# Long FFT convolution feeding a phase mixer: phase steps, evictions and transfers re-placed around the last inverse transform

## The chip, the cores and the metric

The kernel runs on one core of a Trainium2 chip. The metric is device time in microseconds of that core, as the median of repeated executions of the whole program. The kernel before was executed eight times: median 2128.61 us, lowest 2123.54, highest 2137.8.

## The reference, cut to what matters

There are two layers. The first is a causal long convolution along the sequence, done with a Fourier transform of twice the length:

```python
batch, seq, d_model = 8, 5696, 128
Y = rfft(x, n=2*seq, axis=1) * rfft(h, n=2*seq, axis=0)
y = irfft(Y, n=2*seq, axis=1)[:, :seq, :]
```

The second takes y as its input. It forms an angle for every token and channel, rotates, mixes the tokens with two seq x seq matrices, and ends with a small channel layer:

```python
theta = y @ w_theta
zr, zi = y * cos(theta), y * sin(theta)
u = y + w_tok_r @ zr + w_tok_i @ zi      # over tokens, per batch and channel
out = u + relu(u @ w_ch)
```

The two token matrices hold 2 x 5696 x 5696 numbers in float32, and every one of them is read from HBM. Inputs and output are float32; inside, the kernel works in f16 (transforms) and bf16 (mixing).

## The kernel before, in words

**Convolution.** The work is cut into eight groups: four pairs of batches (bp) by two halves of the channels (dh). Each group passes four stages. Stages a and b (`stage_a`, `stage_b`) transform forward and multiply with the transform of h; stages c and d (`stage_c`, `stage_d`) transform back. Stage c of a group has 16 chunks of 16 matmuls, each evicted from PSUM into the tile `g`. Stage d has 7 chunks (six of 10 and one of 4 columns), each evicted into the tile `yt` (line 349). When a group's `yt` is whole it is written to HBM as `yt_hbm` (line 355). The loop at line 594 weaves the back transform of one group with the forward transform of the next. The last group has no next one; its place is taken by phase steps.

**Phase steps.** `phase_step(ti, hh)` handles one tile of 128 tokens for four batches (hh is 0 for batches 0 to 3, 1 for batches 4 to 7). It transposes y on TensorE (L569), computes the angle with two rounds of matmuls (L399 to L405), copies y out of PSUM on VectorE (L574), takes absolute value, sine and cosine on ScalarE (L410, L411, L412), multiplies on VectorE (L423, L424), and sends out y (`y2_hbm`, L575) and the two products (`z_hbm`, L441, or for some tokens straight into the mixing operand, L437). The y copies use six slots in turn, the products seven (`zz`). There are 22 steps for hh = 0 (`steps0`) and 22 for hh = 1 (`steps1`). Of `steps0`, ten are woven into stage c of the last group, six into its stage d (lines 598 and 609), and six follow (line 660). `steps1` are woven into the first stretch of the mixing (line 988, `next_steps`).

**What phase steps read.** y of batches 0 to 3 comes back from HBM into `ya0` (line 534). y of batches 4 to 7 goes into `ya1`: three parts from HBM (lines 544 and 546), and the last half of the channels of batches 6 and 7 directly from the last group's `yt` in SBUF, two transfers on SyncE's queue (SP's, line 549). `stage_d` calls this last load (`then`) and directly after it sends the rest of `yt` to HBM on GpSimd's (POOL's) queue.

**Mixing.** 44 tiles of tokens are handled in two passes over the reduction, with seven products per pair of tiles. The first pair (i = 1, 2, 3 in the loop at line 892) is done plainly, with four products. The operand made of z is held in eleven tiles `b0` to `b10`. The first seven are loaded in half from `z_hbm` on POOL's queue (line 639), which waits for the `steps0` that made them; the other half, and tiles 7 and 8, are completed by the direct writes of `steps1` (L437). Tiles 9 and 10 are loaded by `open_mixing` (line 680), after the last of `steps1`, on SP's queue. The token matrices arrive through a ring of six buffers on POOL's queue (L501): `ring["upto"]` says how many loads may be issued, `pump` issues those that may go and whose buffer has been read. Four addends of the first pair (`cs`, `addend`) are read back from `y2_hbm` and `yt_hbm` on SP's queue (lines 810 and 814), and `tc.issue_after` puts them behind the last load of `open_mixing`.

**What sets the order.** Each engine runs its own instructions in one fixed order. A planner in the framework makes that order: the program's order is its priority, but it may bring an instruction forward that it takes to be ready. `tc.issue_after(ins)` adds an edge: what is issued in its block on the same engine comes after `ins`. PSUM holds four buffers of two banks during the convolution and the `steps0`.

Of the kernel before, what the change touches and what calls it, by code (L numbers as in the profile page):

```python
# [22 lines left out]
def kernel(  # L23
# [310 lines left out]
    def stage_d(st, bp, dh, then=None):  # L334
        def chunk(n0, cn):
            if n0 == 0:
                st["yt"] = fg.tile([P, NB, N2], BF16, tag="yt", name="yt")
            g_, yt = st["g"], st["yt"]
            ps = psum()
            nq = 5 if cn == CN else cn  # L340
            for j in range(cn):
                n = n0 + j
                o = ps[:, j // nq, (j % nq) * NB:(j % nq + 1) * NB]
                for ri in range(2):
                    e_ = e_t[:K1, n, ri, :] if n < EN else e_t[:K1, N2 - n, ri, ::-1]
                    nc.tensor.matmul(o, g_[:K1, ri * N2 + n, :], e_, start=(ri == 0), stop=(ri == 1))
            y_out = yt[:, :, n0:n0 + cn].rearrange("p m (a q) -> p m a q", q=nq)
            y_in = ps[:, :cn // nq, :nq * NB].rearrange("p a (q m) -> p m a q", q=nq)
            nc.scalar.activation(y_out, y_in, AF.Copy)
            if n0 + cn == N2:  # L350
                if then is not None:
                    then(yt)
                for e in range(2):
                    t0 = H if then else 0
                    (nc.gpsimd if then else nc.sync).dma_start(
                        yt_hbm[dh * HD:(dh + 1) * HD, 2 * bp + e, t0:],
                        yt[64 * e:64 * e + 64].rearrange("p m n -> p (m n)")[:, t0:])
        return [lambda n0=n0, cn=cn: chunk(n0, cn) for n0, cn in CHN]

    zz_n, ZB = [0], 3  # L360
# [112 lines left out]
    def pump():  # L473

        while (ring["n"] < len(queue) and (ring["n"] < 6 or queue[ring["n"] - 6][0] in ring["read"])
               and ring["n"] < ring["upto"]):
            queue[ring["n"]][1]()
# [6 lines left out]
    def small(at, n):  # L484
        return ring["all"][:, WB + BT + at:WB + BT + at + n]
# [100 lines left out]
    def with_load(step, load):  # L586
        def both():
            step()
            if load:
                ring["upto"] += 1  # L590
                pump()
        return both

    for g, (bp, dh) in enumerate(groups):
        st = {}
        last = g + 1 == len(groups)
        a_, load_, b_ = front(g + 1)
        now = [with_load(steps0.pop(0), 2 < n < 9) for n in range(10)] if last else []
        c_ = stage_c(st, last)
        if dh == 0 and bp + 1 < B // 2:  # L600
            def next_x(bp=bp):
                x16s[bp + 1] = load_x(bp + 1)
            a_ = a_ + [next_x]
        woven((c_, 0.06 if a_ else 0.0, 1.0), (a_, 0.0, 0.35 if dh == 0 else 0.55), now, load_)
        if g + 2 == len(groups):
            xin.close()
            open_phases()
            load_ya0()
        now = [steps0.pop(0) for _ in range(6)] if last else []
        woven(b_, (stage_d(st, bp, dh, load_ya1 if last else None), 0.0, 1.1 if b_ else 1.0), now)  # L610
        if g + 2 == len(groups):
            load_ya1()
            open_ring()
# [59 lines left out]
    def open_mixing():  # L673

        nonlocal bp, cp, wlp, ybp
        pha.close()
        xa.close()
        bp, cp, wlp, ybp = (ctx.enter_context(tc.tile_pool(name=name, bufs=bufs, reuse_waits="tile"))
                            for name, bufs in (("bpool", 1), ("cpool", 1), ("wlpool", 2), ("ybpool", 3)))
        for j in range(len(bts_of[0]), NJ):  # L680
            load_b(0, j, bp, nc.sync)
        spread.extend(bg_phase(t, h) for t in list(range(24, 34)) + [22, 23, 44] + list(range(34, 44)) for h in range(2))
        spread.extend(bg_left(g) for g in range(0, NT, 4))

# [207 lines left out]
    for i, (k, p, tt, j0, s0, nj) in enumerate(stretches):  # L892
# [67 lines left out]
                for n in range(2):  # L960
                    nc.sync.dma_start(wl[n], wl_hbm[:, 22 * n + tt, :])
        if j0 + s0 == (3 if classic else 2) * TJ:
            with tc.issue_after(sides["late"].ins) if p == 0 and tt == 0 else ExitStack():
                cs = [addend(p, n, t, h) for n, (t, h) in enumerate(where)]

        def aside(first_of, second_of):
            nonlocal second
# [20 lines left out]
        if i == 1:  # L988
            for q, (h, s) in enumerate(((0, 0), (0, 1), (1, 0), (1, 1))):
                for n in range(4):  # L990
                    for j in range(TJ):
                        product((held, a)[s], s * TJ + j, j, n, (h,))
                        if (n * TJ + j) % 2:
                            next_steps(1)
                    if n % 2 and q == 1:
                        ring["upto"] += 1
                        pump()
                    if q == 3 and n == 0:
                        ring["upto"] = len(queue)
                        nxt = prepare(2)  # L1000
            continue
        if i == 2:
            for h in range(2):
# [119 lines left out]
```

## Time and profile before

| What | Value |
|---|---|
| median of eight executions | 2128.61 us |
| the profiled execution, its own time | 2125.64 us |
| span of its instructions | 2123.7 us |
| TensorE busy | 1993.8 us (94%) |
| VectorE busy | 1597.9 us (75%) |
| ScalarE busy | 675.2 us (32%) |
| GpSimd busy, mostly issuing transfers | 908.6 us (43%) |
| granted TensorE clock, mean | 0.972 |

Busy time is summed over the span; an engine's share says little about a single stage. The part that this document is about lies between 385 and 535 us from the span's start: last chunks of the seventh group until 391, stage c of the last group from 393 to 423, stage d to 441, the last `steps0` to 452, and the first stretches of the mixing after that. From 540 us on TensorE works nearly without a gap until the end. In a row such as "PE L569 MATMUL ... [3.41 <-DMA ya<-yt]" the bracket is the time for which the engine stood idle before the instruction and what it was waiting for.

### The profile page before, as it was taken

To read this page: it belongs to the slowest core of one execution; us is meant where nothing else is said; L and a number is where in the kernel's file an instruction comes from. 1 tells how busy PE (TensorE), PEld (TensorE's weight loads), DVE (VectorE), ACT (ScalarE), POOL (GpSimd) and SP (SyncE) were. 2 spreads that over 40 slices of the span, in tenths; PEclk is the share of its full clock that TensorE was granted. 3 is DMA by queue.
4 is the path that set the end of the run, shared out by engine and by line. 5 is a ranking of instruction groups with operands and counts; after the bars stand their busy time and mean duration, and the time that the engine had idled before them with its cause. 6 is when DMAs were issued, how large, how long until landed. Compare 5 with 4: busy or idle time off the path is not lost.

```text
span 2123.7 us, 41486 instructions
## 1 busy us (share of the span) xinstructions
PE 1993.8 (94%) x15765; PEld 1113.8 (52%) x15765; DVE 1597.9 (75%) x2880; ACT 675.2 (32%) x997; POOL 908.6 (43%) x1661
## 2 busy tenths in 40 slices
PE   3788889787999999999999998999999999999998
PEld 3787888754444444444444443444444444444444
DVE  7867767776778887888886757677777777686867
ACT  4877877884332333232310000011111111111111
POOL 5301011237344636354556543445444454545450
PEclk8699989999999999999999999999999999999999
DMA  6357464889789989898999879777878787969693
GB/s 138 100 131 172 126 166 130 230 251 241 157 152 179 178 173 168 170 177 172 175 174 163 129 152 262 109 138 142 145 135 152 129 153 129 158 121 159 127 155 90
DMA packets 408264, 334.95 MB, mean 158 GB/s; under 512 B 85927, under 2 KB 358439, under 8 KB 407079
## 3 DMA queue, kind: packets, MB, share of 16 engines
q0 software_dynamic: 225952, 156.72, 51.7%
q1 hardware_dynamic: 176128, 164.05, 26.5%
q10 hardware_dynamic: 5984, 11.54, 1.5%
q8 instruction: 123, 2.02, 0.4%
q14 instruction: 77, 0.63, 0.1%
HBM read 377.11 MB, written 92.49 MB: 221 GB/s over the span
## 4 chain that ended last, share of the span: by engine, by line
PE 67%; DMA 2%; DVE 2%; issue 1%; POOL 0%; ACT 0%; DVEq 0%; ACTq 0%; POOLq 0%
PE m L1060 61%; PE m L982 2%; DMA b<-z_hbm 2%; PE v L789 1%; PE utp L782 1%; DVE c L1067 1%; PE m L1064 1%; PE m L936 0%; PE m L934 0%; PE theta_ps L388 0%; PE tpz L730 0%; DVE wt L702 0%; DMA ring<-in_moe_w_tok_r_dram 0%; POOL ring L501 0%; DMA yT<-yt_hbm 0%
## 5 line engine op out<-in xcount | busy, mean ns | idle before, releaser
L501 POOL DMA_DIRECT2D ring<-in_moe_w_tok_i_dram x720 | 388.5, 546 | 679.6 <-DVE wt L702 605.7
L501 POOL DMA_DIRECT2D ring<-in_moe_w_tok_r_dram x720 | 387.3, 545 | 150.6 <-DVE wt L702 88.8
L702 DVE STREAM_TRANSPOSE wt<-ring 128x384 f32<-128x384 f32 (+2 forms) x720 | 360.4, 528 | 103.1 <-PE m L1060 70.7
L1060 PE MATMUL m<-b,wt 128*128 128x512 bf16 x1640 | 388.3, 379 | 2.0 <-DVE wt L702 1.7
L1060 PEld LDWEIGHTS <-wt 128*128 128x128 bf16 x1804 | 176.1, 98 | 215.8 <-DVE wt L702 4.4
L1067 DVE TENSOR_TENSOR c<-c,m 128x512 f32<-128x512 f32 x412 | 267.5, 676 | 0.4 <-PE m L1060 0.4
L784 ACT ACTIVATE ring<-utp 128x512 bf16<-128x512 bf16 (+1 forms) x86 | 51.0, 593 | 608.6 <-PE utp L782 608.6
L323 PE MATMUL ps<-r_u,u_t 128*128 128x128 f16 x1024 | 132.2, 229 | 10.5 <-DVE u_t L307 9.9
L324 PE MATMUL ps<-r_v,v_t 128*128 128x128 f16 x1024 | 131.2, 228 | 0.1
L982 PE MATMUL m<-b,wt 128*128 128x512 bf16 x480 | 112.2, 383 | 10.6 <-DMA b<-zz 6.2
L779 ACT ACTIVATE ub<-c 128x512 bf16<-128x512 f32 (+1 forms) x90 | 56.3, 629 | 198.0 <-DVE c L950 116.2
L129 POOL DMA_DIRECT2D x<-in_x_dram x64 | 34.0, 538 | 189.2 <-PE ps L193 178.5
L323 PEld LDWEIGHTS <-u_t 128*128 128x128 f16 x1024 | 106.2, 104 | 11.9 <-DVE u_t L307 11.9
L324 PEld LDWEIGHTS <-v_t 128*128 128x128 f16 x1024 | 105.3, 103 | 2.9 <-DVE v_t L307 1.3
L305 ACT ACTIVATE xs<-ps 128x1024 f16<-128x1024 f32 x96 | 95.3, 1019 | 13.7 <-DVE v_t L307 7.2
L307 DVE TENSOR_TENSOR u_t<-xs,hs 128x1024 f16<-128x1024 f16 x96 | 71.8, 748 | 28.6 <-ACT xs L305 19.3
L193 PE MATMUL ps<-f_t,x 89*128 89x180 f16 x512 | 81.5, 313 | 9.6 <-ACT xs L305 6.7
L982 PEld LDWEIGHTS <-wt 128*128 128x128 bf16 x528 | 50.4, 99 | 70.5 <-issue 15.3
L211 PEld LDWEIGHTS <-w_t 64*128 64x128 f16 x3240 | 60.4, 102 | 39.6 <-issue 25.3
L193 PEld LDWEIGHTS <-x 89*128 89x128 f16 x512 | 73.3, 233 | 11.5 <-issue 10.8
L390 ACT ACTIVATE red<-theta_ps,magic 128x512 f32<-128x512 f32 (+1 forms) x46 | 31.7, 688 | 134.8 <-PE theta_ps L388 113.7
L732 ACT ACTIVATE ring<-tpz 128x512 bf16<-128x512 bf16 (+1 forms) x46 | 27.5, 598 | 136.4 <-PE tpz L730 118.4
(2889 smaller groups left out, 3887.8 us busy)
## 6 DMA issues: line engine op xcount, KB each, us to landing
ring<-in_moe_w_tok_r_dram POOLq DMA_DIRECT2D x352, 96.0 KB, 4.3
ring<-in_moe_w_tok_i_dram POOLq DMA_DIRECT2D x352, 96.0 KB, 4.7
ring<-in_moe_w_tok_r_dram POOLq DMA_DIRECT2D x352, 80.0 KB, 4.4
ring<-in_moe_w_tok_i_dram POOLq DMA_DIRECT2D x352, 80.0 KB, 3.7
hs<-hf_hbm SPq DMA_DIRECT2D x192, 128.0 KB, 3.2
cp_hbm<-c SPq DMA_DIRECT2D x88, 256.0 KB, 2.5
c<-cp_hbm SPq DMA_DIRECT2D x88, 256.0 KB, 4.3
out_dram<-c SPq DMA_DIRECT2D x88, 256.0 KB, 4.3
```

The costliest lines, as they stand in the source:

```text
L193: nc.tensor.matmul(ps[:, i // 2, (i % 2) * 2 * K1:(i % 2 + 1) * 2 * K1], lhs(q + i), f1_t[:NB], start=True, stop=True)
L211: nc.tensor.matmul(ps[:, e, j * HD:(j + 1) * HD], w_t2[rows, c0 + j, N2 * (1 - ri):N2 * (3 - ri)], a_st["a"][rows, ri * K1 + c0 + j, :], s ...
L305: nc.scalar.activation(xs[:, :, :, :ck], ps, AF.Copy)
L307: nc.vector.tensor_tensor(uv[r][:, :, :, c0:c0 + ck], xs[:, :, :, :ck], hv[:, r:r + 1, :, :ck].to_broadcast([P, 2, HD, ck]), op=mult)
L323: nc.tensor.matmul(o, u_t[:, at:at + P], r_u, start=True, stop=False)
L324: nc.tensor.matmul(o, v_t[:, at:at + P], r_v, start=False, stop=True)
L501: nc.gpsimd.dma_start(wb[32 * i:32 * i + 32, :ng, :nj * 64], bass.AP(tensor=a.tensor, offset=a.offset + row0 * S + p * H + i * QR + j0 * 6 ...
L702: nc.vector.transpose(wt.rearrange("p j t r -> p (j t r)").bitcast(F32).rearrange("p (j g t) -> p g j t", j=TJ, g=4)[:, :ng, :nj], wb[:, : ...
L779: nc.scalar.activation(ub[:m].rearrange("p b d -> p (b d)"), c[:m], AF.Copy)
L982: nc.tensor.matmul(ms[n // 2 * 2 + h], a[n][:, j, :, r], bts_of[p][jj][n % 2 * 2 + h][:, r, :], start=(n % 2 == 0 and jj == 0 and r == 0), ...
L1060: nc.tensor.matmul(ms[q], a[q][:, j, :, r], bts[jj][q][:, r, :], start=(jj == 0 and r == 0), stop=(jj == NJ - 1 and r == 1 and q not in left))
L1067: nc.vector.tensor_tensor(c, z, ms[q], op=op)
```

## The change

The change has five parts.

1. Three of the `steps0` are traced ahead of stage c of the last group. Nine instead of ten are then woven into stage c, five instead of six into stage d, and five instead of six follow. The six loads of the ring stay attached to the same steps (the fourth to the ninth).
2. In stage d of the last group, the second, fourth and sixth of the seven evictions move from ScalarE to VectorE (a copy).
3. After the last group's `yt` is whole, GpSimd copies one element of `ya1`, from the end of the second load of line 549, into scratch space. The two transfers that send the rest of `yt` to HBM are put behind that copy on GpSimd's queue.
4. In `open_mixing` the four addends are requested between the loads of tiles 9 and 10 of the operand, instead of later and behind both.
5. In the first stretch of the mixing (i = 1) the remaining ring loads are released at the end of the stretch instead of a quarter of the way into its last part.

```diff
@@ stage_d, chunk
-            nc.scalar.activation(y_out, y_in, AF.Copy)
+            if then is not None and n0 // CN % 2:
+                nc.vector.tensor_copy(y_out, y_in)
+            else:
+                nc.scalar.activation(y_out, y_in, AF.Copy)
             if n0 + cn == N2:
                 if then is not None:
                     then(yt)
+                if then is not None:
+                    gate = nc.gpsimd.tensor_copy(small(0, 1)[HD:HD + 1], sides["phases"][1][HD:HD + 1, 3, H - 1:H]).ins
                 for e in range(2):
                     t0 = H if then else 0
-                    (nc.gpsimd if then else nc.sync).dma_start(
-                        yt_hbm[dh * HD:(dh + 1) * HD, 2 * bp + e, t0:],
-                        yt[64 * e:64 * e + 64].rearrange("p m n -> p (m n)")[:, t0:])
+                    with tc.issue_after(gate) if then else ExitStack():
+                        (nc.gpsimd if then else nc.sync).dma_start(
+                            yt_hbm[dh * HD:(dh + 1) * HD, 2 * bp + e, t0:],
+                            yt[64 * e:64 * e + 64].rearrange("p m n -> p (m n)")[:, t0:])
@@ the loop over the groups
-        now = [with_load(steps0.pop(0), 2 < n < 9) for n in range(10)] if last else []
+        if last:
+            for _ in range(3):
+                steps0.pop(0)()
+        now = [with_load(steps0.pop(0), n < 6) for n in range(9)] if last else []
         c_ = stage_c(st, last)
...
-        now = [steps0.pop(0) for _ in range(6)] if last else []
+        now = [steps0.pop(0) for _ in range(5)] if last else []
@@ open_mixing
-        for j in range(len(bts_of[0]), NJ):
-            load_b(0, j, bp, nc.sync)
+        load_b(0, NJ - 2, bp, nc.sync)
+        sides["cs"] = [addend(0, n, t, h) for n, (t, h) in enumerate(((0, 1), (22, 0), (0, 0), (22, 1)))]
+        load_b(0, NJ - 1, bp, nc.sync)
@@ the mixing
         if j0 + s0 == (3 if classic else 2) * TJ:
-            with tc.issue_after(sides["late"].ins) if p == 0 and tt == 0 else ExitStack():
-                cs = [addend(p, n, t, h) for n, (t, h) in enumerate(where)]
+            cs = (sides["cs"] if p == 0 and tt == 0 else
+                  [addend(p, n, t, h) for n, (t, h) in enumerate(where)])
...
                     if q == 3 and n == 0:
-                        ring["upto"] = len(queue)
                         nxt = prepare(2)
+            ring["upto"] = len(queue)
+            pump()
             continue
```

## The prediction

> **What bounds the kernel now.** First the busy times by stage: TensorE (the first figure) is nearly full from 540 us on, and has holes before.
>
> ```profile
> core 0: us, PE busy (x) PEld busy (x) DVE busy (x) ACT busy (x) POOL busy (x), PEclk, DMA share, GB/s
> 390.00:400.00 10.00, 6.94 (x81) 6.09 (x82) 4.44 (x8) 3.86 (x9) 4.09 (x8) 0.66 1.05 282
> ...
> 430.00:440.00 10.00, 9.02 (x142) 7.34 (x140) 7.03 (x14) 10.00 (x18) 0.00 (x0) 1.00 0.70 161
> 440.00:450.00 10.00, 5.99 (x73) 4.34 (x69) 9.15 (x19) 10.00 (x20) 1.13 (x2) 0.90 0.85 211
> ...
> 510.00:520.00 10.00, 5.13 (x18) 1.92 (x16) 4.09 (x8) 0.00 (x0) 8.05 (x16) 0.83 1.12 204
> ...
> 540.00:550.00 10.00, 10.00 (x54) 4.80 (x53) 4.60 (x9) 3.74 (x6) 2.18 (x4) 1.00 1.08 197
> ```
>
> The timeline of TensorE says what each large hole waited for:
>
> ```profile
> 393.06 0.29 PE L323 MATMUL ps<-r_u,u_t 128*128 128x128 f16 x1 [4.02 <-DVE u_t L307]
> ...
> 423.46 1.13 PE L346 MATMUL ps<-e_t,g__8355 90*128 90x89 f16 x20 [2.30 <-ACT red L411]
> ...
> 447.92 0.37 PE L569 MATMUL tpz<-ident_bf,ya 128*128 128x128 bf16 x3 [2.09 <-ACT red L411]
> 451.70 0.29 PE L569 MATMUL tpz<-ident_bf,ya 128*128 128x128 bf16 x1 [3.41 <-DMA ya<-yt]
> ...
> 459.29 0.59 PE L982 MATMUL m<-b,wt 128*128 128x512 bf16 x2 [1.88 <-DMA b<-z_hbm]
> ...
> 467.97 0.38 PE L569 MATMUL tpz<-ident_bf,ya 128*128 128x128 bf16 x4 [1.77 <-DVE ring L574]
> ...
> 516.66 6.85 PE L982 MATMUL m<-b,wt 128*128 128x512 bf16 x24 [4.87 <-DMA b<-zz]
> ...
> 531.07 0.38 PE L1025 MATMUL m<-yy,ident_bf 128*128 128x512 bf16 x1 [2.27 <-DMA yy<-y_hbm]
> ```
>
> All holes from 386 to 535 add up to about 31 us; that is the most the change can win. Between 395 and 452 ScalarE is the limit: 10.0 of 10.0 us busy at 430 and 440 us, while VectorE has 7.0 at 430. The chain from there is: last eviction of stage d (until 441.8), second load of `ya1` (issued at 446.1, landed 451.6), first of `steps1` at 451.7. From 452 to 512 TensorE runs with small holes; at the end it waits for the last direct write into the operand. The waits name two transfers that hold SP's queue, and POOL's timeline names what stands before that write:
>
> ```profile
> SPq L546 <- DMA yt_hbm<-yt: 6.8, 1, 6.8
> SPq L628 <- DMA b<-zz: 9.2, 1, 9.2
> ```
> ```profile
> 505.50 1.07 POOL L437 DMA_DIRECT2D b<-zz  x2
> 506.56 2.21 POOL L501 DMA_DIRECT2D ring<-in_moe_w_tok_r_dram  x4
> 508.74 2.19 POOL L501 DMA_DIRECT2D ring<-in_moe_w_tok_i_dram  x4
> 511.82 0.58 POOL L575 DMA_DIRECT2D y_hbm<-ring  x1 [0.90 <-DMA ring<-in_moe_w_tok_r_dram]
> 513.46 1.08 POOL L437 DMA_DIRECT2D b<-zz  x2 [1.06 <-DMA ring<-in_moe_w_tok_r_dram]
> ```
>
> Eight ring loads (4.4 us of issuing) stand between the last but one step's transfers and the last step's, though VectorE had finished the last step at 505.1.
>
> **What the Trainium skill says.** *TensorE: Matmul & The Clock Gate*, section "What's actually happening": after an idle window of about 3.4 us the array runs at half clock, until about 3.4 us of work. The trace agrees: after the hole of 4.02 us matmuls follow at 0.107 us until 396.9, then at 0.055. *VectorE: DVE Perf Modes*, section "Why PSUM operands drop a tier": a float32 source in PSUM goes one element per cycle. The rows agree (below). *DMA: Bandwidth & Descriptors*, section "Anatomy of one DMA — SWDGE (gpsimd) path": DMA engines wait on no semaphore, the issuing queue does, so what stands behind a waiting request waits too. The 9.2 us of L628 above show it; the gate uses it on purpose.
>
> **Part 1, three steps into the hole.** A step costs TensorE 1.1 us (397.77 to 398.88), ScalarE 1.66 (0.48 + 0.57 + 0.61, start to start at 401.03), VectorE 1.55 (0.33 + 0.61 + 0.61). `ya0` was issued by 371 us and landed within 8.0, the mixing ring's memory is free at 387. So three steps, 3.3 us on TensorE, fit between 389.0 and 393.1, and stage c then starts with a warm clock (1.9 us better from 393.06 to 396.88). On ScalarE they fill the hole of 4.33 us before 395.20. ScalarE's work from 390.9 to the first stage d eviction is now 12 steps and 8 evictions of 1.06: 19.9 + 8.5 = 28.4 us, against 33.7 us elapsed before (10 steps, with 8.6 us of holes). I leave 2.2 us of small waits, a quarter of those before: stage d starts 3.1 earlier. Against it: the first step's y cannot leave before SP's queue is free of L546 (401.3), lands near 405.7 (3.7 median), and the seventh step needs its slot near 404. I charge 1.0 (bounds 0 and 1.7). Gain **2.1 us**.
>
> **Part 2, three evictions on VectorE.** Before, stage d took 18.3 us (423.5 to 441.8): 7 evictions (5.1) and 6 steps (10.0) on ScalarE. Now ScalarE has 4 evictions, 2.75, and 5 steps, 8.3: 11.1. VectorE gets three of 128x890 from PSUM in float32; no such row exists here, but 128x720 costs 0.901 (L198) and 90x1024 1.215, so about 1.06 each: 3.2 + 5 x 1.55 = 10.9. TensorE needs 128 x 0.055 + 5 x 1.1 = 12.6 and becomes the limit. With 0.6 for the last eviction: 13.2. Gain **5.1 us**. If VectorE's order is bad (an eviction standing behind a product that waits for ScalarE, 0.8 each time), 2.4 of it go.
>
> **Then `ya1`.** From stage d's end to landing were 9.8 us, the two loads being apart on SP by two z writes; I leave that. `steps1` start 7.2 us earlier, near 444.5. The five remaining steps don't cover more: ScalarE's 2.75 + 10 x 1.66 = 19.4 us from 421.5 end at 441.
>
> **Part 3, the gate.** Before, POOL issued the `yt` transfers at 442.1 and the operand's half tiles (L639) at 452.4, 0.7 us after `steps1` could start. Now the copy (0.3, row L499 1x1) and two issues (1.1) come between: 1.2 us later relative to `ya1`. Queued behind are twelve L639 (6.6 us) and after them `steps1`'s y writes, on which the slots depend. The 0.72 MB of `yt` now also compete with those loads, 2.9 us at 250 GB/s; `ya1` may land sooner without them. Loss **2.0 us** in the wait of 459.29 (bounds 0 and 4). In return SP's y and z writes of `steps0` finish earlier relative to `steps1` (before, they lasted until 463), so of the 1.77 us at 467.97 I take back **1.0** (bounds 0 and 1.8).
>
> **Parts 4 and 5.** The last step's two writes follow at once on POOL, issued at 507.1 to 508.2 in the old time, landed by 511 (3.1 us, as at 514): TensorE, busy until 511.8, loses none of its 4.87 us. Tile 10 waited for the same write, so its load moves by about as much. The addends, four issues of 0.4 to 1.4 us, fit into SP's idle 9.2 us; their wait of 2.27 goes. I charge 1.0 for tile 10 behind them. Gain **6.1 us** (bounds 2 and 8.9, which includes tile 10's own 1.32 and 0.41). The ring loads come 1.7 us later in POOL's order and are wanted by VectorE at 524.8 to 527.4, where it waited 1.08 already; TensorE is covered there by products of tiles already transposed until after 540, so I charge nothing; if the cover is gone, up to 1.7.
>
> **Sum.** 2.1 + 5.1 - 2.0 + 1.0 + 6.1 = 12.3 us. The profiled execution took 2125.6, so 2113.3; it lay 3.0 below the median of the runs shown, so the median goes to **2116.0**. Its own range is 2110 to 2122.
>
> **Rivals.**
> - *Transfers bound the front.* The DMA share is 0.95 to 1.15 in most slices from 390 to 530. If the half tiles land when they did, the front keeps only 1 us and the tail 5: 2122.5. Against it: 0.70 and 0.85 at 430 to 450, and the bytes are the same.
> - *All waits fall together.* No slot stall, no loss at the gate, tile 10's waits gone, `ya1`'s loads adjacent on SP (3 us): about 20 us, 2108.
> - *The planner undoes it.* Before, it put only half a transposition ahead of stage c's second matmul; if it brings stage c's work and POOL's ring loads forward again, nothing moves but 1 us: 2127.5.
> - *Slower: POOL held at the gate.* If SP's queue puts the second `ya1` load behind the writes of all later steps, the gate holds L639 and the y writes, the slots run out, VectorE stands and TensorE with it. It decides when `ya1` lands after about 465 (452, plus the 6.1 of the tail and 1.0 that it must eat, plus 6.4 to be measurably slower); for 2136 it must land near 466. Against it: five steps put only 15 writes of 0.6 us on SP.
>
> **How the numbers follow.** A measurement of this kernel tells 0.3% (6.4 us) from no change: faster is below 2122.2, slower above 2135.0. Chances: the sum 0.46; transfers 0.20, half of it below the line; all waits 0.14; undone 0.10; gate 0.10. Faster 0.46 + 0.10 + 0.14 = 0.70; same 0.20; slower 0.10. The range from 2104 (all waits, with a median 4 below) to 2131 (undone, 3.5 above) leaves out the gate case and little else.
>
> **What would show it.** Right: no hole of 4 us at 393 and three steps there; stage d about 13 us with ScalarE below 9 of 10; `ya1` landing near 444; L437's last write directly behind the one before; no wait of L1025. Wrong: a hole of VectorE for `y_hbm<-ring` in stage c; `ya1` landing later than 450; L982 waiting over 6 us for `z_hbm`; tile 10 waiting for the addends' queue; or new holes after 540 us, which I expect nowhere.

## The result and the profile after

The changed kernel takes 2122.51 us (median of 21 runs, 2117.71 to 2127.77), the kernel before 2129.47 (58 runs); the ratio is 0.9968, with a 95% interval of 0.9960 to 0.9977. The gain is 6.8 us where the prediction had 12.3. The profiled execution spans 2115.0 us, against 2123.7.

Parts are numbered as in the section on the change: 1 the early steps, 2 the evictions, 3 the gate, 4 the addends, 5 the release. Line numbers are those of the kernel whose trace is shown. Lines up to L348 have the same number as before; later ones move by 3 to 11 (L569 is now L575, L982 is L992, L1025 is L1036).

The windows view of the kernel after:

```profile
core 0: us, PE busy (x) PEld busy (x) DVE busy (x) ACT busy (x) POOL busy (x), PEclk, DMA share, GB/s
390.00:400.00 10.00, 6.96 (x92) 5.46 (x91) 7.55 (x15) 7.09 (x15) 2.65 (x5) 1.00 1.07 284
430.00:440.00 10.00, 9.41 (x141) 7.62 (x139) 8.38 (x15) 8.47 (x16) 0.00 (x0) 1.00 0.73 170
440.00:450.00 10.00, 5.75 (x46) 3.93 (x44) 9.86 (x20) 9.80 (x18) 1.60 (x3) 0.72 0.95 227
510.00:520.00 10.00, 9.04 (x42) 3.83 (x40) 9.01 (x15) 0.00 (x0) 5.37 (x11) 1.00 1.19 267
```

ScalarE is no longer full at 430 (10.00 before), and TensorE has 9.04 us of work at 510 where it had 5.13. TensorE's timeline gives the holes that are left:

```profile
392.69 0.23 PE L323 MATMUL ps<-r_u,u_t 128*128 128x128 f16 x1 [0.82 <-DVE u_t L307]
424.17 1.00 PE L346 MATMUL ps<-e_t,g__8436 90*128 90x89 f16 x20 [2.16 <-DVE g__8436 L331]
444.23 0.33 PE L575 MATMUL tpz<-ident_bf,ya 128*128 128x128 bf16 x3 [2.09 <-DMA z_hbm<-zz]
446.30 0.29 PE L575 MATMUL tpz<-ident_bf,ya 128*128 128x128 bf16 x1 [1.75 <-DMA ya<-yt]
459.08 1.86 PE L992 MATMUL m<-b,wt 128*128 128x512 bf16 x4 [2.99 <-DMA b<-z_hbm]
501.50 10.71 PE L992 MATMUL m<-b,wt 128*128 128x512 bf16 x41 [3.29 <-DVE wt L712]
512.98 5.99 PE L992 MATMUL m<-b,wt 128*128 128x512 bf16 x27 [0.34 <-DMA b<-zz]
524.94 0.59 PE L1036 MATMUL m<-yy,ident_bf 128*128 128x512 bf16 x2
```

The hole of 4.02 us at 393 is 0.82 now, the wait for the last direct write (4.87) is 0.34, and the addend's (2.27) is gone. But stage d does not begin sooner (424.17 against 423.46). `steps1` does (446.30 against 451.70); its 5.4 us have vanished by 459.08, where TensorE waits 2.99 us for a half tile at the time at which it did before (459.29). A new wait of 3.29 us stands at the end of the first stretch.

Two instructions mark how far the work has come: the end of the last product of the first stretch (the 96th L992) and the start of the first product of the part where seven products are woven (L1071). They stand at 506.38 and 567.11 after, 505.31 and 574.52 before. So at the end of the first stretch the kernel after is 1.1 us *late*, and it wins 8.5 us in the following 60. After that it wins about 1 more: 1547.9 against 1549.2 us to the end. These are two single executions; what the parts are worth is read from the repeated times below.

### The profile page after: what moved, and what is told of

Same layout as the page of the kernel before. It is cut to its first block, busy times and chain, and to the rows that moved or that the text cites. A ratio compares the mean times of both kernels' runs of the same rounds, so it can differ in the third digit from the quotient of the medians.

```text
span 2115.0 us, 41486 instructions
## 1 busy us (share of the span) xinstructions
PE 1998.0 (94%) x15765; PEld 1114.4 (53%) x15765; DVE 1599.3 (76%) x2883; ACT 673.1 (32%) x994; POOL 909.3 (43%) x1662
## 3 DMA queue, kind: packets, MB, share of 16 engines
q1 hardware_dynamic: 176128, 164.05, 26.6%
## 4 chain that ended last, share of the span: by engine, by line
PE 67%; DMA 2%; DVE 2%; issue 1%; POOL 0%; ACT 0%; DVEq 0%; ACTq 0%; POOLq 0%
PE m L1071 60%; PE m L992 2%; DMA b<-z_hbm 2%; PE v L799 1%; PE utp L792 1%; PE m L1075 1%; DVE c L1078 1%; PE m L946 0%; PE m L944 0%; DVE wt L712 0%; POOL ring L507 0%; PE theta_ps L394 0%; PE tpz L740 0%; DMA wl<-in_moe_w_tok_i_dram 0%; DMA z_hbm<-mag 0%
## 5 line engine op out<-in xcount | busy, mean ns | idle before, releaser
L712 DVE STREAM_TRANSPOSE wt<-ring 128x384 f32<-128x384 f32 (+2 forms) x720 | 360.5, 528 | 111.3 <-PE m L1071 67.5
L1071 PE MATMUL m<-b,wt 128*128 128x512 bf16 x1640 | 388.3, 379 | 2.0 <-DVE wt L712 1.7
L1071 PEld LDWEIGHTS <-wt 128*128 128x128 bf16 x1804 | 176.1, 98 | 215.5 <-DVE wt L712 4.4
L992 PE MATMUL m<-b,wt 128*128 128x512 bf16 x480 | 114.3, 388 | 7.3 <-DMA b<-z_hbm 3.7
L307 DVE TENSOR_TENSOR u_t<-xs,hs 128x1024 f16<-128x1024 f16 x96 | 70.6, 736 | 30.8 <-ACT xs L305 20.2
L992 PEld LDWEIGHTS <-wt 128*128 128x128 bf16 x528 | 51.1, 100 | 66.8 <-issue 9.7
L801 DVE SCALAR_TENSOR_TENSOR c<-v,c 128x512 f32<-128x512 f32 (+1 forms) x90 | 61.8, 689 | 11.2 <-PE v L799 11.2
```

The lines of the kernel that those rows point to most:

```text
L307: nc.vector.tensor_tensor(uv[r][:, :, :, c0:c0 + ck], xs[:, :, :, :ck], hv[:, r:r + 1, :, :ck].to_broadcast([P, 2, HD, ck]), op=mult)
L712: nc.vector.transpose(wt.rearrange("p j t r -> p (j t r)").bitcast(F32).rearrange("p (j g t) -> p g j t", j=TJ, g=4)[:, :ng, :nj], wb[:, : ...
L801: nc.vector.scalar_tensor_tensor(c[:m], v[:m], 0.0, c[:m], op0=ALU.max, op1=ALU.add)
L992: nc.tensor.matmul(ms[n // 2 * 2 + h], a[n][:, j, :, r], bts_of[p][jj][n % 2 * 2 + h][:, r, :], start=(n % 2 == 0 and jj == 0 and r == 0), ...
L1071: nc.tensor.matmul(ms[q], a[q][:, j, :, r], bts[jj][q][:, r, :], start=(jj == 0 and r == 0), stop=(jj == NJ - 1 and r == 1 and q not in left))
```

## The experiments

Twelve kernels, on three chips, each beside the kernel before on the same chip; so it is the ratios that can be compared, not the medians. All but `e9` and `e11` hold some of the five parts and nothing else.

| kernel | parts | median us | ratio to before, 95% interval |
|---|---|---|---|
| after | 1 2 3 4 5 | 2122.5 | 0.9968 [0.9960, 0.9977] |
| e1_front | 1 2 3 | 2131.9 | 1.0013 [1.0004, 1.0022] |
| e2_tail | 4 5 | 2120.0 | 0.9956 [0.9939, 0.9974] |
| e3_nogate | 1 2 4 5 | 2121.4 | 0.9966 [0.9952, 0.9980] |
| e4_release | 5 | 2125.1 | 0.9982 [0.9973, 0.9991] |
| e5_noevict | 1 3 4 5 | 2121.3 | 0.9960 [0.9946, 0.9975] |
| e6_nosteps | 2 3 4 5 | 2122.9 | 0.9968 [0.9957, 0.9980] |
| e8_tail_evict | 2 4 5 | 2118.0 | 0.9948 [0.9934, 0.9962] |
| e9_yt_sync | 2 4 5, `yt` on SyncE | 2121.9 | 0.9968 [0.9955, 0.9981] |
| e11_gate_first | 1 to 5, earlier gate | 2124.8 | 0.9977 [0.9965, 0.9989] |
| e12_tail_gate | 3 4 5 | 2124.4 | 0.9978 [0.9970, 0.9987] |
| e13_tail_steps | 1 4 5 | 2121.9 | 0.9965 [0.9952, 0.9978] |
| e14_addends | 4 | 2126.7 | 0.9990 [0.9978, 1.0002] |

### The front and the tail apart

Parts 1, 2 and 3 alone:

```diff
-        load_b(0, NJ - 2, bp, nc.sync)
-        sides["cs"] = [addend(0, n, t, h) for n, (t, h) in enumerate(((0, 1), (22, 0), (0, 0), (22, 1)))]
-        load_b(0, NJ - 1, bp, nc.sync)
+        for j in range(len(bts_of[0]), NJ):
+            load_b(0, j, bp, nc.sync)
...
+                        ring["upto"] = len(queue)
                         nxt = prepare(2)
-            ring["upto"] = len(queue)
-            pump()
             continue
```

> Parts 1, 2 and 3 alone (early steps, evictions on VectorE, gate); the addends and the release of the ring loads stay as before. In the changed kernel the first of steps1 comes 5.4 us earlier than before (446.3 against 451.7), but the product that ends the first stretch comes 1.1 us later. Queue theory (the gate and what now stands ahead of the half tiles on GpSimd's queue eat the front's gain): no faster than before, 2127 to 2131 us, half tiles first issued at 454, not before 452. Transfer theory (the DMA engines are full from 450 to 505, whatever the queue): the same time, so these two aren't told apart here. Sum theory (the gains add as the prediction had them): 6 us faster than before, near 2123.

Parts 4 and 5 alone (the gate is taken out as well; the diff is cut):

```diff
-            if then is not None and n0 // CN % 2:
-                nc.vector.tensor_copy(y_out, y_in)
-            else:
-                nc.scalar.activation(y_out, y_in, AF.Copy)
+            nc.scalar.activation(y_out, y_in, AF.Copy)
...
-        if last:
-            for _ in range(3):
-                steps0.pop(0)()
-        now = [with_load(steps0.pop(0), n < 6) for n in range(9)] if last else []
+        now = [with_load(steps0.pop(0), 2 < n < 9) for n in range(10)] if last else []
```

> Parts 4 and 5 alone (addends between tiles 9 and 10, ring loads released at the end of the stretch); the front stays as before. If the whole gain is made in the tail: 7 to 8.5 us faster than before, as fast as the whole change or a little faster, 2121 to 2122. Sum theory: 6.1 us faster, 2123, with the change of the front adding as much again.

Measured: the front alone makes the kernel slower by 0.13%, 2.8 us (0.9 to 4.7); the tail alone makes it faster by 0.44%, 9.4 us (5.5 to 13.0). The two add up to 6.6, the 6.8 of the whole. All of the gain comes from the tail, and the front gives some of it back. The prediction had counted 6.2 us for the front and 6.1 for the tail. Of the expectations, the sum theory fails for the front; for the tail the interval holds both forecasts, though the median lies beyond them.

The front alone also shows where part 1 stops. The first line is VectorE's timeline of this kernel, the second ScalarE's:

```profile
399.28 0.39 DVE L307 TENSOR_TENSOR u_t<-xs,hs 128x256 f16<-128x256 f16 x1 [3.43 <-DMA hs<-hf_hbm]
```
```profile
400.33 0.60 ACT L416 ACTIVATE mag<-ps 128x512 f32<-128x512 f32 x1 [6.18 <-DVE ring L580]
```

ScalarE, whose hole the three steps were to fill, waits 6.18 us for the first step's copy of y (L580). That copy stands on VectorE behind the last product of L307, and that one waits for the last load of `hs`. The kernel after has the same order with a shorter wait:

```profile
392.24 0.39 DVE L307 TENSOR_TENSOR u_t<-xs,hs 128x256 f16<-128x256 f16 x1 [1.45 <-DMA hs<-hf_hbm]
392.54 0.39 DVE L307 TENSOR_TENSOR v_t<-xs,hs 128x256 f16<-128x256 f16 x1
392.84 0.75 DVE L580 COPY ring<-ps 128x512 bf16<-128x512 bf16 x2
```
```profile
393.30 0.60 ACT L416 ACTIVATE mag<-ps 128x512 f32<-128x512 f32 x1 [2.91 <-DVE ring L580]
```

The steps' matmuls did run in the hole (from 388.37), but their ScalarE work began at 393.30, when the hole was over. The hole ends with a wait for `hs`, and stage c cannot begin before `hs` is there.

### Without the gate

```diff
-                if then is not None:
-                    gate = nc.gpsimd.tensor_copy(small(0, 1)[HD:HD + 1], sides["phases"][1][HD:HD + 1, 3, H - 1:H]).ins
...
-                    with tc.issue_after(gate) if then else ExitStack():
-                        (nc.gpsimd if then else nc.sync).dma_start(
+                    (nc.gpsimd if then else nc.sync).dma_start(
```

> The whole change without part 3: no gate, the two transfers of yt go out on GpSimd's queue as soon as yt is whole. Queue theory: the half tiles are issued before 450, TensorE's wait of 2.99 us at 459 goes, and 2 to 4 us are gained on the changed kernel, 2118 to 2120. Transfer theory: ya1 lands later because yt's writes compete with it, the products start no earlier, and the time is that of the changed kernel or up to 2 us more, 2122 to 2125.

Measured: 2121.4 us, 0.9966, not told from the whole change and between the two forecasts. In its profile the second load lands 12.5 us after stage d's end, against 9.6 with the gate, and `steps1` starts later, as the transfer theory has it; but POOL is free sooner and its first half tile goes at 451.07 instead of 454.27, which is still later than the 450 of the queue theory. One is worse and the other better, so this run alone could not say what the gate is worth.

### The release alone

```diff
                     if q == 3 and n == 0:
-                        ring["upto"] = len(queue)
                         nxt = prepare(2)
+            ring["upto"] = len(queue)
+            pump()
             continue
```

> Part 5 alone on the kernel before: only the release of the ring loads moves to the end of the first stretch. If the last direct write behind eight ring loads was the tail's main wait: 4 to 5 us faster than before, 2124 to 2125, with the wait of 2.27 us for the addend left. If tile 10 and the addends set the tail's end: under 2 us.

Measured: 0.9982, 3.8 us (1.9 to 5.7), close to the 4 to 5 of the first forecast. The waits of this kernel from 504 to 576 us (engine and line, what it waited for, us in total, times, longest):

```profile
PE m L1026 <- DMA yy<-y_hbm: 2.7, 1, 2.7
PE m L982 <- DMA b<-zz: 1.9, 1, 1.9
...
DVE ring L644 <- DMA y_hbm<-ring: 1.2, 1, 1.2
```

The wait for the direct write has fallen to 1.9 us (4.9 in the same view before), and VectorE's wait for the write of y, which had stood behind the ring loads on POOL, to 1.2 (5.8 before). The addend's wait is untouched.

### The addends alone

```diff
-        for j in range(len(bts_of[0]), NJ):
-            load_b(0, j, bp, nc.sync)
+        load_b(0, NJ - 2, bp, nc.sync)
+        sides["cs"] = [addend(0, n, t, h) for n, (t, h) in enumerate(((0, 1), (22, 0), (0, 0), (22, 1)))]
+        load_b(0, NJ - 1, bp, nc.sync)
...
+            cs = (sides["cs"] if p == 0 and tt == 0 else
+                  [addend(p, n, t, h) for n, (t, h) in enumerate(where)])
```

> Part 4 alone: the four addends and the order of the last loads, the release left as before. The tail was 9.4 us better and the release alone 3.8, so if the two add: 5 to 6 us better than before, 2123 to 2124.5 us, with the waits for the addend and the second tile of block 1 gone and those for the ring's tiles left. If the release only pays once the addends are there (or the other way round), part 4 alone gives under 3 us (2126 us or more) or over 8 us (2121 us or less).

Measured: 0.9990, 2.1 us, with an interval that reaches to nothing. The same view:

```profile
PE m L983 <- DMA b<-zz: 6.1, 1, 6.1
...
DVE ring L644 <- DMA y_hbm<-ring: 6.4, 1, 6.4
```

Here the addend's wait is gone and the direct write's stands, 6.1 us long. So each part removes its own wait, as the prediction had it. Both of them stand one after the other on TensorE's way through the same 60 us. Alone the two gained 2.1 and 3.8, together 9.4. The result for the addends alone is the one that was expected where either part pays fully only beside the other. The profiles point the same way: from the end of the first stretch to the first of the woven seven products takes 67.9 us with the release alone, 67.2 with the addends alone, 69.2 and 67.5 in the two kernels with neither, and 62.5 on average (60.1 to 65.1) in the ten with both. But these are single executions, and 5.9 lies within the interval of the 9.4 (5.5 to 13.0), so this is likely and not shown.

### Which part of the front costs

With parts 4 and 5 always there, five more kernels, with those above, give all eight ways to take parts 1, 2 and 3. Without the early steps (2, 3, 4, 5):

```diff
-        if last:
-            for _ in range(3):
-                steps0.pop(0)()
-        now = [with_load(steps0.pop(0), n < 6) for n in range(9)] if last else []
+        now = [with_load(steps0.pop(0), 2 < n < 9) for n in range(10)] if last else []
...
-        now = [steps0.pop(0) for _ in range(5)] if last else []
+        now = [steps0.pop(0) for _ in range(6)] if last else []
```

> Parts 2, 3, 4 and 5, without the three phase steps ahead of the last group. So far the front (parts 1 to 3 alone) costs 2.8 us and the tail (parts 4 and 5 alone) gains 9.4 us against 2128.9. Steps theory (the early steps cost: their copies stand on VectorE behind the product that waits for the last load of hs, and ScalarE waits with them): without them the front's loss goes, stage c begins again about 4 us after the last inverse of the group before it, and the time is 2116 to 2120 us. Supply theory (the first stretch of products ends by what POOL, the ring and the half tiles supply, whatever the front does): no gain from the evictions, 2119 to 2121 us. Gate theory (the gate on POOL lets y transfers ahead of the half tiles, and that costs): 2121 to 2124 us, no better than the whole change at 2122.

Without the evictions (1, 3, 4, 5):

```diff
-            if then is not None and n0 // CN % 2:
-                nc.vector.tensor_copy(y_out, y_in)
-            else:
-                nc.scalar.activation(y_out, y_in, AF.Copy)
+            nc.scalar.activation(y_out, y_in, AF.Copy)
```

> Parts 1, 3, 4 and 5, without the three evictions on VectorE. Stage d lasts 18 us again in place of 12.5 us. Evictions theory (they are what helps in the front): 5 us worse than the whole change, 2126 to 2128 us. Supply theory (the time that stage d gives is not passed on): within 1.5 us of the whole change, 2121 to 2124 us. Steps theory says nothing more than that it is not better than the tail alone (2120 us).

The evictions and the tail (2, 4, 5), both edits of `e6_nosteps` and `e3_nogate` together. This diff and the next two are against `e2_tail`:

```diff
-            nc.scalar.activation(y_out, y_in, AF.Copy)
+            if then is not None and n0 // CN % 2:
+                nc.vector.tensor_copy(y_out, y_in)
+            else:
+                nc.scalar.activation(y_out, y_in, AF.Copy)
```

> Parts 2, 4 and 5: the tail and the evictions, neither the early steps nor the gate. Steps theory: 2115 to 2118 us, since the evictions shorten stage d by 5 us and the loss of the steps is absent. Supply theory: 2119 to 2121 us, as the tail alone. Gate theory: better by 2 us or more than the same kernel with the gate. With the gate gone the four writes of yt go ahead of or beside the loads that the second half's steps wait for, so these begin 60 us or more after the last inverse of group 6 where the kernel with everything had 58.

The gate and the tail (3, 4, 5):

```diff
+                if then is not None:
+                    gate = nc.gpsimd.tensor_copy(small(0, 1)[HD:HD + 1], sides["phases"][1][HD:HD + 1, 3, H - 1:H]).ins
...
+                    with tc.issue_after(gate) if then else ExitStack():
```

> Parts 3, 4 and 5: the gate added to the tail, neither early steps nor evictions. Together with the other runs on the same tail it gives every one of the eight ways to take parts 1, 2 and 3. Queue theory: the gate costs 2 to 4 us against the tail alone, so 2121 to 2124 us, with the first half tile 31 us or more after stage d's first product. If the gate costs nothing by itself: 2119 to 2121 us.

The steps and the tail (1, 4, 5):

```diff
-        now = [with_load(steps0.pop(0), 2 < n < 9) for n in range(10)] if last else []
+        if last:
+            for _ in range(3):
+                steps0.pop(0)()
+        now = [with_load(steps0.pop(0), n < 6) for n in range(9)] if last else []
...
-        now = [steps0.pop(0) for _ in range(6)] if last else []
+        now = [steps0.pop(0) for _ in range(5)] if last else []
```

> Parts 1, 4 and 5: the early steps added to the tail, neither gate nor evictions. Steps theory (the early steps' copies stand on VectorE behind the product that waits for hs; ScalarE gains nothing from them and the last group's stage d comes 1 to 2 us later): 2 to 4 us worse than the tail alone, 2121 to 2124 us. Part 1 as the prediction had it (2.1 us to the good, if it is passed on): 2117 to 2119 us. Neither: 2119 to 2121 us.

The gain of each over before, in us, (1 - ratio) x 2129:

| with parts 4, 5 and | no gate | gate |
|---|---|---|
| neither 1 nor 2 | 9.4 | 4.7 |
| 2, evictions | 11.1 | 6.8 |
| 1, steps | 7.5 | 8.5 |
| 1 and 2 | 7.2 | 6.8 |

Each cell is uncertain by 2 to 4 us, so single differences say little; the mean over four against four is better, about 2.0 us either way (worked out from the eight intervals). With the gate the mean is 6.7, without it 8.8: it costs 2.1 us. Steps: 7.5 with, 8.0 without; evictions: 8.0 with, 7.5 without. So the gate costs about 2 us on average, just more than the uncertainty; the steps and the evictions, which were to gain 2.1 and 5.1, gain nothing that these runs can tell. The average hides a difference: without the steps the gate costs 4.5 us (both upper rows), with them it gains 0.3 (both lower rows), and in the whole change against `e3_nogate` it costs 0.4, give or take 3.5. The two averages differ by 4.8, give or take 3.9; this was noticed in the table and not forecast. Of the expectations, the gate theory holds for `e6` (2122.9) and the queue theory for `e12`, just above its upper end (2124.4, half tiles 31.8 us after stage d's first product); the supply theory holds for `e5` (2121.3) and misses `e8` (2118.0) by 1, where the gate theory holds too (4.9 us better than `e6`). The steps theory fits `e8` and `e13` (2121.9), the two without the gate, but not `e6`, and not the mean over all eight. Where the steps go in ScalarE's order can be seen in the profiles: with the steps stage d begins on average 2.6 us later after the end of group 6 (37.8 us in six kernels, 35.2 in eight), and by then two steps more are done, which is 3.3 us of ScalarE's work.

Stage d's length shows why parts 1 and 2 were thought to be a pair. From its first product to the last eviction: 18.2 to 18.5 us with neither (before, `e2`, `e4`, `e14`; 17.1 with the gate, `e12`), 16.3 with the evictions alone (`e6`, `e8`, `e9`), 16.5 and 16.6 with the steps alone (`e13`, `e5`), 12.5 with both and the gate (after, `e1`, `e11`) and 14.1 with both and no gate (`e3`). The shortening is real, and yet it buys nothing that the times show. The next two runs ask why.

### `yt` on SyncE, and a gate that opens earlier

The two writes of `yt` on SyncE's queue, behind the second load (with parts 2, 4, 5):

```diff
-                    (nc.gpsimd if then else nc.sync).dma_start(
+                    nc.sync.dma_start(
                         yt_hbm[dh * HD:(dh + 1) * HD, 2 * bp + e, t0:],
```

> As parts 2, 4 and 5, with the two writes of yt to the HBM on SyncE's queue, right behind the second load that comes out of yt, in place of POOL's. POOL is then free of them and the half tiles can be issued earlier. If POOL's order and issue time set the end of the first stretch: 2113 to 2117 us, 2 us or more better than the same kernel with the writes on POOL. If not (supply from the HBM or the engines sets it): the same within 1.5 us. If SyncE's queue is the tighter one, the z writes behind the two yt writes come later and the half tiles wait for them: 2 us or more worse.

Measured: 2121.9 us, 0.9968, against 0.9948 with the writes on POOL. Freeing POOL of the two writes moved the first half tile by nothing (452.65 us against 453.20): it waits for a z write of `steps0` to land, not for POOL. POOL's timelines of `e8` and of this kernel:

```profile
453.20 4.92 POOL L642 DMA_DIRECT2D b<-z_hbm  x9 [11.34 <-DMA z_hbm<-zz]
```
```profile
452.65 4.29 POOL L642 DMA_DIRECT2D b<-z_hbm  x8 [27.54 <-DMA z_hbm<-zz]
```

(It is not the last of these writes; that one is issued at 463.65 and 463.63.) So POOL's order is not what holds it when there is no gate, and the forecast of 2113 to 2117 us for that case fails. By its median the kernel is 4 us worse than `e8`, as the third forecast has it, though the intervals overlap; SyncE has the two writes (2.06 us) ahead of the later z writes of `steps0`.

The whole change with the gate on the first load in place of the second:

```diff
-                    gate = nc.gpsimd.tensor_copy(small(0, 1)[HD:HD + 1], sides["phases"][1][HD:HD + 1, 3, H - 1:H]).ins
+                    gate = nc.gpsimd.tensor_copy(small(0, 1)[HD:HD + 1], sides["phases"][1][HD:HD + 1, 2, H - 1:H]).ins
```

> The whole change, its gate on the first of the two loads that come out of yt in place of the second. In the profile of the change POOL was held by the gate to 446.31 us, then sent the two writes of yt, and one write to the ring and two y writes before the first half tile, which came 30.1 us after stage d's first product; without the gate that was 27.3 us, with it 30.1 to 33.2 in four kernels. Queue theory (what the gate costs is POOL's order: y transfers ahead of the half tiles): POOL is through with yt 2 to 4 us earlier and fewer y transfers stand ahead of the half tiles, so that these begin 28 to 29.5 us after stage d's first product, and the time is 2118 to 2121 us. Traffic theory (the gate helps because yt's bytes stay away from the second load): the second load lands 2 us or more later and the time is no better, 2122 to 2125 us.

POOL's timeline of the kernel before, of the kernel after, and then of this one, with the idle time before each:

```profile
442.06 1.13 POOL L355 DMA_DIRECT2D yt_hbm<-yt  x2 [16.60 <-ACT yt L349]
452.41 4.91 POOL L639 DMA_DIRECT2D b<-z_hbm  x9 [9.22 <-DMA z_hbm<-zz]
```
```profile
446.31 0.48 POOL L357 COPY ring<-ya 1x1 bf16<-1x1 bf16 x1 [24.05 <-DMA ya<-yt]
446.87 1.12 POOL L361 DMA_DIRECT2D yt_hbm<-yt  x2
450.10 0.58 POOL L581 DMA_DIRECT2D y_hbm<-ring  x1 [2.11 <-DVE ring L580]
451.49 0.56 POOL L443 DMA_DIRECT2D ring<-zz  x1 [0.81 <-DVE zz L430]
452.04 0.57 POOL L581 DMA_DIRECT2D y_hbm<-ring  x1
454.27 4.26 POOL L648 DMA_DIRECT2D b<-z_hbm  x8 [1.66 <-PE theta_ps L411]
```
```profile
447.46 0.22 POOL L357 COPY ring<-ya 1x1 bf16<-1x1 bf16 x1 [23.13 <-DMA ya<-yt]
448.02 1.12 POOL L361 DMA_DIRECT2D yt_hbm<-yt  x2 [0.34 <-ACT mag L416]
454.32 0.58 POOL L581 DMA_DIRECT2D y_hbm<-ring  x1 [5.18 <-DMA y_hbm<-ring]
455.10 1.08 POOL L648 DMA_DIRECT2D b<-z_hbm  x2 [0.20 <-issue]
```

The three transfers between `yt` and the half tiles in the kernel after are `steps1`'s own; with the gate late, they come ahead of the half tiles in the order. Opened earlier, the gate leaves one of them there, and the half tiles begin 26.7 us after stage d's first product, as soon as in any of the kernels (26.8 in `e13`). The second load lands no later for it (9.5 us after stage d's end, 9.6 in the kernel after), so the traffic theory has the right time for a wrong reason. The queue theory has its step right (fewer transfers ahead, half tiles even sooner than it said) and the time wrong: 0.9977 is no better than the whole change. Why this kernel is not faster stays open.

### What the first stretch ends by

All fourteen profiles together, each counted from stage d's first product because the stages before it scatter by some us from execution to execution: the start of `steps1`, the issue of the first half tile that POOL has to send then (the first of twelve; tile 0 went out in stage c), the end of the first stretch. In eight of the profiles 10 to 17 of the 528 records of these matmuls are missing, but none of their weight loads, so the end of the stretch is taken from the matmul that follows the 96th weight load.

| kernels | `steps1` starts | first half tile | stretch 1 ends |
|---|---|---|---|
| before | 28.2 | 28.9 | 81.9 |
| after | 22.1 | 30.1 | 82.2 |
| no gate on the second load, late start (e2, e4, e8, e14) | 27.4 to 28.3 | 28.1 to 29.0 | 81.8 to 83.5 |
| no gate, earlier start (e3, e9, e13) | 25.3 to 26.6 | 26.8 to 29.5 | 80.1 to 83.3 |
| gate on the second load (e1, e5, e6, e12) | 22.2 to 25.8 | 30.3 to 33.2 | 82.9 to 86.6 |
| gate on the first load (e11) | 22.1 | 26.7 | 82.9 |

Over the fourteen, the end of the stretch goes with the first half tile (correlation 0.78; 0.85 with the landing of the twelfth) and not with the start of `steps1` (-0.24). An early start of 6 us never came out as an early end; with the gate on the second load (five profiles against eight without a gate) the half tiles are on average 2.9 us later and the end 2.3 us later, the size of its 2.1 us in the times. A correlation is no proof, and in `e11` early half tiles brought no early end. That the start of `steps1` doesn't set the end is what these profiles show; what else sets it, once the half tiles are there, was not tested. There are two candidates.

POOL's queue is one: it is full at the end of the stretch in both kernels, 9.78 and 10.00 of 10 us from 490 and 500 before, 9.03 and 10.00 after. In the kernel after, what ends in the 3.29 us at 501.50 passes through a wait for a write of y, which POOL sends (VectorE's timeline):

```profile
499.15 0.42 DVE L580 COPY ring<-tpz 128x512 bf16<-128x512 bf16 x1 [2.21 <-DMA y_hbm<-ring]
```

TensorE's own pace is the other. The first wait for a half tile ends at 459.29 before and at 459.08 after. From about there to the end of the stretch, before and then after (columns as in the windows view above):

```profile
459.00:505.31 46.31, 41.60 (x359) 25.48 (x359) 35.82 (x67) 34.17 (x58) 36.62 (x67) 1.00 0.95 279
459.00:506.38 47.38, 43.38 (x328) 24.91 (x328) 31.35 (x58) 30.02 (x51) 37.72 (x69) 0.90 0.93 261
```

The kernel after has 31 matmuls fewer left to do, and yet TensorE is busy for 1.8 us more, because the granted clock is 0.90 on average and not 1.00: after the wait of 2.99 us four products take 1.86 us (459.08), where four from 467.27 take 1.03. In this trace, then, the earlier start meets a longer wait for the half tile, and slower matmuls behind the wait. The six kernels with a gate all waited 2.7 to 4.4 us for this half tile, and from there to the end of the stretch a slower clock cost them 3.0 to 5.9 us (the length of that part times what the clock lacked of 1.00); the eight without waited 0.8 to 1.9 us, and it cost them 0 to 3.4. No run keeps the clock up while all else stays, so this is a candidate, not the cause shown.

## Why the prediction was right and where it was wrong

The median, 2122.5, lies in the range of 2104 to 2131, and 6.5 us above the 2116.0 (2116.3, if its last addition is done again). It lies just outside the 2110 to 2122 that the sum gave for itself, and 0.3 us above the 2122.2 that it drew as the line to "faster", to which it had given a chance of 0.70. That more than half of the gain came is in part luck: the front, counted at plus 6.2 us, cost 2.8, and the tail, counted at 6.1, gave 9.4. Step by step:

- **Part 1, "they fill the hole of 4.33 us" on ScalarE: wrong.** The working took TensorE's and ScalarE's free time and `ya0`'s landing into account, but not what stands ahead of the steps' copies on VectorE: the products that wait for `hs`. ScalarE was to begin at 390.9 and began at 393.30; its work up to stage d then took the 28.3 us that were counted (28.4). What was right is the warm clock: stage c's products come at 0.055 to 0.06 us from 393.06, at once, as *TensorE: Matmul & The Clock Gate* ("What's actually happening") of the Trainium skill would have it. The wait of 2.99 us that is left at 459.08, shorter than the page's about 3.4, was followed by slow matmuls all the same. The warm start moved nothing, as TensorE does not set the start of stage d. In the eight kernels without the early steps the first product of stage d waits for ScalarE (2.30 us before); in five of the six with them it waits for VectorE's eviction of `g` (2.16 after). VectorE, whose 1.55 us a step the sum for stage c left out, was busy for 27.3 of the 31.3 us before that product, ScalarE for 28.3. Stage d was to start 2.1 us earlier, all charges taken, and started 0.7 later in the profile.
- **Part 2, stage d of 13.2 us: right.** It lasted 12.5, with 1.08 us for an eviction on VectorE (1.06 expected) and TensorE busy for 11.9 of the 12.5, the limit as forecast; though only together with part 1: 16.3 alone.
- **`ya1`, 9.8 us after stage d: right.** 9.6. `steps1` started 5.4 us earlier: 5.8 from the shorter stage d and 0.3 from the landing, less the 0.7 by which stage d began later. But the last `steps0`, which were to end on ScalarE at 441 and so ahead of it, ended at 448.14, after `steps1` had begun at 446.30; before, they ended at 451.83. So only 3.7 of the 5.4 us could reach ScalarE.
- **Part 3, a loss of 2.0 us (0 to 4) and 1.0 taken back: of this size on average,** 2.1 plus or minus 2.0, where the net forecast was 1.0; beside the steps no cost is seen. The wait for the half tiles grew where it was put (1.88 us before, 2.99 after), and it came from more than the copy and the issues: three transfers of `steps1` went ahead of the half tiles as well. TensorE's waits for the copies of y, of which 1.0 was to go, fell from 2.3 us to 0.6 between 444 and 516.
- **The sum, which carried the 7.2 us to the end: the step that failed.** It supposed that the first stretch keeps its length, so that an earlier start is an earlier end. The stretch took 53.6 us before and 60.1 after, from the start of `steps1` to its last product: 1.0 of the 6.5 is more idle time of TensorE, and 5.5 is the same 402 matmuls, transpositions included, done at a granted clock of 0.87 in place of 0.97. The longer wait for the half tile was priced (2.0), the slower pace after a wait was not. What sets the end of the stretch stays open. The gain of 5.1 was real up to 446 us, and was worth nothing at 506. The first rival, which ended at 2122.5, had this consequence, and the number; its own reason, that transfers bound the front, is not shown. Its half tiles were to land when they did; the first wait for one ended at 459.08, against 459.29, and the twelfth landed at 470.0, against 467.2.
- **Parts 4 and 5, 6.1 us: right in the cause, low in size.** From the end of the first stretch to the first of the woven seven products takes 62.5 us on average in the ten kernels with both parts and 69.2 and 67.5 in the two with neither, a gain of 5.9. In times the tail alone gained 9.4, and the whole against the front alone 9.6, both above the upper bound of 8.9; where the other 3.5 us are won, the profiles don't show. The waits went as stated: 4.87 to 0.34, 2.27 to nothing, and tile 10's 1.32 and 0.41, which were in the upper bound, to 0.70.
- **The later ring loads, charged at nothing: right.** VectorE waits for them up to 3.57 us at 525, TensorE then for VectorE 0.63 at most up to 540, and after that as long as before (1.7).
- **The other rivals.** POOL held at the gate needed a landing near 465; it landed at 446.3. The planner did not undo it. Nothing opened after 540 us.

No kernel here is shown to beat the changed one. The tail with the evictions and without gate and steps (`e8_tail_evict`, 2118.0 us, 0.9934 to 0.9962) is the best by its ratio, and its interval touches that of the change (0.9960 to 0.9977).

## What to carry to other kernels

An earlier start of a stage is worth only what its last supplier lets through: before adding the gain of one stage to that of the next, name what ends the later stage and ask whether that supplier moves too. Filling a hole of one engine takes all the engines of the filling work: look at the order of each of them for an instruction that waits for the same thing that made the hole. Here two small reorderings of transfers at a point where TensorE stood waiting gave everything, and the three edits that shortened the way to a stretch that did not end by its start gave nothing that the runs can tell; together they cost 2.8 us. And where an earlier start only makes TensorE wait longer, count the slower matmuls after the wait as well: here 43.38 us busy for 328 of them, where 41.60 had done 359.

## What the runs showed of the hardware

A one-element copy on GpSimd makes a prompt gate: it ran at 446.31 us where the load had landed at 446.26, and at 447.46 after a landing at 447.41, 0.05 us each. What stands behind it on the queue waits with it: POOL was idle for 24.05 us ahead of the gate, where 16.60 had passed ahead of the same two writes before. A DMA issue occupied POOL for 0.53 to 0.58 us in all of the lines above, so an order of three transfers ahead of others is worth 1.7 us even when none of them waits. TensorE's matmuls slowed to half pace after a wait of 2.99 us: four of 128x512 took 1.86 us from 459.08 and 1.03 from 467.27. And in single profiled executions the seventh group's last inverse ends anywhere from 385.6 to 392.2 us (387.9 to 390.1 in the eight kernels without early steps), so that times within a profile had to be compared from a point near the change.
